# A two-token attention decode step: one load stream through a ring of 2-MB slots, and PE work interleaved by groups of eight

## The chip, the core and the metric

The kernel runs on one core of a Trainium2 chip. The metric is device time in microseconds (us) of one execution. Engines are named as the profile names them: PE (matmuls; PEld is its weight load), DVE, ACT, POOL, and SP, which here only issues transfers. Sixteen DMA engines move the data between HBM and the core's memory (SBUF); matmuls write to PSUM.

## The reference

```python
def _A_ref(x, k_cache, v_cache, wq, wo):          # x 2x1x512, caches 2x32x8192x128
    q = (x @ wq).reshape(B, Sq, H, Dh)            # heads H = 32, Dh = 128
    scores = einsum("bhqd,bhkd->bhqk", q, k_cache) * (Dh ** -0.5)
    o = einsum("bhqk,bhkd->bhqd", softmax(scores), v_cache)
    return o.reshape(B, Sq, H * Dh) @ wo
...
def _B_ref(x, w1, w2):                            # w1 512x1792, w2 1792x512
    return relu(x @ w1) @ w2
...
xn = layernorm(x)
return x + _A_ref(xn, k_cache, v_cache, wq, wo) + _B_ref(xn, w1, w2)
```

All arrays are bf16. The two caches are 2 x 134 MB and are read once. The weights wq and wo have 4.19 MB each, w1 and w2 1.84 MB each.

## The kernel before

There are 64 pairs of batch and head, called heads below. The cache of one head is one transfer of 2 MB for K and one of 2 MB for V, 16 KB per partition, both issued by SP (`issue_k_dma`, `issue_v_dma`). K has 3 buffers and V has 4. The weights and x are issued by ACT, wq and w1 at the start, w2 and wo after the first products with them.

A head takes these steps. `transpose_phase` turns 64 blocks of K on PE (`tp`, L204) in 8 groups of 8, and each group is copied from PSUM to SBUF (`kt_`), six by DVE and two by ACT. `qk_phase` multiplies each turned block with the query, written 64 times side by side (`qbt`), so the 64 matmuls have 64 columns (`S`, L235), and takes the row maximum (`mcol`). `stats_tr` turns that column on PE (`tr`) and DVE takes the maximum (`mx`). `stats_exp` spreads it over the partitions by a matmul (`bcp`), ACT negates it (`NM`) and takes the exponential with its row sums (`Psb`, `RS`). `stats_den` sums over the partitions on PE (`dbp`), and DVE takes the reciprocal (`RD`). `pv_phase` runs 64 matmuls of V with the probabilities (`ot`, L283), and ACT scales the result (`OTn`). `wo_phase` multiplies with that head's part of wo into one accumulator (`fin`, L299). After all heads, 14 matmuls add the second product of B (L328), DVE adds x (`osb`), and SP writes it out.

The loop `for it in range(NBH + 3)` calls the phases of up to four heads, but the order of the instructions on an engine is set by a scheduler when the kernel is built, not by this text.

Of the kernel before, what the change touches and what calls it, by code (L numbers as in the profile page):

```python
# [24 lines left out]
def kernel(  # L25
# [33 lines left out]

    const = ctx.enter_context(tc.tile_pool(name="const", bufs=1))  # L60
    wbig = ctx.enter_context(tc.tile_pool(name="wbig", bufs=1))
    wff = ctx.enter_context(tc.tile_pool(name="wff", bufs=1))
    kpool = ctx.enter_context(tc.tile_pool(name="kpool", bufs=K_BUFS))
    vpool = ctx.enter_context(tc.tile_pool(name="vpool", bufs=V_BUFS))
    kts = ctx.enter_context(tc.tile_pool(name="kts", bufs=KTS_BUFS))
    small = ctx.enter_context(tc.tile_pool(name="small", bufs=4))
    psT = ctx.enter_context(tc.tile_pool(name="psT", bufs=PST_BUFS, space=bass.MemoryType.PSUM))
    psS = ctx.enter_context(tc.tile_pool(name="psS", bufs=1, space=bass.MemoryType.PSUM))
    psO = ctx.enter_context(tc.tile_pool(name="psO", bufs=1, space=bass.MemoryType.PSUM))
    psM = ctx.enter_context(tc.tile_pool(name="psM", bufs=1, space=bass.MemoryType.PSUM))  # L70
    psF = ctx.enter_context(tc.tile_pool(name="psF", bufs=1, space=bass.MemoryType.PSUM))

    ksb_tiles = {}
    vsb_tiles = {}

    def issue_k_dma(bh):
        if bh >= NBH:
            return
        b, h = bh // H, bh % H
        ksb = kpool.tile([P, KB, Dh], bf16, name="ksb")  # L80
        nc.sync.dma_start(
            ksb[:], A_k_cache[b, h].rearrange("(m kk) d -> m kk d", m=P)
        )
        ksb_tiles[bh] = ksb

    def issue_v_dma(bh):
        if bh >= NBH:
            return
        b, h = bh // H, bh % H
        vsb = vpool.tile([P, KB, Dh], bf16, name="vsb")  # L90
        nc.sync.dma_start(
            vsb[:], A_v_cache[b, h].rearrange("(m kk) d -> m kk d", m=P)
        )
        vsb_tiles[bh] = vsb
# [19 lines left out]
    nc.scalar.dma_start(w1_sb[:], B_w1.rearrange("(kt p) f -> p kt f", p=P))

    for bh in range(PF):
        issue_k_dma(bh)
        issue_v_dma(bh)

    stats = const.tile([Bsz, nc.vector.BN_STATS_DIM], f32, name="stats")  # L120
# [247 lines left out]
```

## Time and profile before

| | |
|---|---|
| timed runs | 733.4, 733.94 and 735.46 us; median 733.94 us |
| the profiled execution, first to last instruction (its span) | 731.9 us |
| between that span and the median of the runs | 2.0 us |
| PE busy | 580.9 us (79% of the span) |
| DVE, ACT busy | 292.6 us (40%), 192.4 us (26%) |
| moved by DMA | 282.25 MB, 386 GB/s over the span |

No own time of the profiled execution stands beside its span, so the 2.0 us to the median are taken as what lies around it. The busy shares are means over the span; where a stage waits is seen in the chain of work and in the windows.

### The profile page before, as it was taken

Reading aid. Unit: us, or ns where it says so; the run is one execution under the profiler, and the core shown is the slowest. Engines: PE = TensorE matmul, PEld = TensorE weight load, DVE = VectorE, ACT = ScalarE, POOL = GpSimd, SP = SyncE. Lnnn points to the kernel's source line nnn. Section 1 sums busy time; section 2 is a strip of 40 time slices with the busy share of each in tenths; the row PEclk is TensorE's granted clock in tenths of the full one; section 3 lists DMA queues with packets and bytes.
Section 4 is the critical chain, followed back from the end, with each engine's and each line's share of the span. In section 5 each row is a group of like instructions: output and inputs, shape, how many; then the busy total and the mean of one; then the engine's idle time right before and its main releaser. Section 6 shows DMA issues by size and latency. Waiting matters only on the chain.

```text
span 731.9 us, 27513 instructions
## 1 busy us (share of the span) xinstructions
PE 580.9 (79%) x12810; PEld 531.1 (73%) x12810; DVE 292.6 (40%) x655; ACT 192.4 (26%) x433; POOL 4.5 (1%) x9
## 2 busy tenths in 40 slices
PE   3273998888888888888888888888888888888887
PEld 3262988778777877777777778777877777787775
DVE  3020454434334434443443344434434442444342
ACT  1032333222222222222222222222222222222221
POOL 2000000000000000000000000000000000000000
PEclk9565999999999999999999999999999999999999
DMA  9999999999999999999999999999999999999920
GB/s 368 429 420 372 370 424 428 424 426 424 407 407 411 408 388 394 396 399 409 390 424 417 363 385 417 402 394 420 399 392 383 407 405 402 373 416 415 398 118 2
DMA packets 25529, 282.25 MB, mean 386 GB/s; under 512 B 2116, under 2 KB 8008, under 8 KB 8520
## 3 DMA queue, kind: packets, MB, share of 16 engines
q1 hardware_dynamic: 18436, 268.45, 89.6%
q10 hardware_dynamic: 6980, 12.06, 4.6%
q8 instruction: 100, 1.64, 0.9%
q14 instruction: 13, 0.11, 0.0%
HBM read 280.50 MB, written 0.00 MB: 383 GB/s over the span
## 4 chain that ended last, share of the span: by engine, by line
PE 78%; ACT 8%; DMA 4%; DVE 4%; issue 4%; another core or an unknown queue 1%; ACTq 1%; DVEq 0%
PE tp L204 32%; PE ot L283 17%; PE S L235 17%; DMA wq_sb<-in_A_wq_dram 4%; ACT Psb L264 3%; PE dbp L275 3%; PE fin L299 3%; ACT OTn L290 2%; DVE mx L254 2%; PE tr L252 2%; DVE mcol L244 2%; ACT NM L263 1%; PE bcp L262 1%; PE qp L169 1%
## 5 line engine op out<-in xcount | busy, mean ns | idle before, releaser
L204 PE MATMUL tp<-identb,ksb 128*128 128x128 bf16 x4096 | 252.7, 223 | 22.2 <-DMA ksb<-in_A_k_cache_dram 19.2
L204 PEld LDWEIGHTS <-ksb 128*128 128x128 bf16 x4096 | 236.5, 100 | 36.9 <-DMA ksb<-in_A_k_cache_dram 19.3
L283 PE MATMUL ot<-Psb,vsb 128*128 128x64 bf16 x4096 | 136.4, 193 | 2.5 <-issue 2.5
L283 PEld LDWEIGHTS <-vsb 128*128 128x128 bf16 x4096 | 133.6, 99 | 3.6 <-issue 2.8
L275 PEld LDWEIGHTS dbp<-RS,onesf 128*128 128x128 f32 x128 | 19.3, 189 | 73.8 <-ACT Psb L264 73.1
L275 PE MATMUL dbp<-RS,onesf 128*128 128x1 f32 x128 | 24.6, 261 | 44.7 <-ACT Psb L264 43.7
L290 ACT ACTIVATE OTn<-ot,RD 128x1 bf16<-128x1 f32 x64 | 16.9, 263 | 150.5 <-PE ot L283 150.5
L276 DVE RECIPROCAL RD<-dbp 128x1 f32<-128x1 f32 x64 | 10.8, 168 | 106.7 <-PE dbp L275 106.7
L244 DVE TENSOR_REDUCE mcol<-S 128x1 bf16<-128x64 f32 x64 | 14.5, 227 | 89.3 <-PE S L235 89.3
L299 PE MATMUL fin<-wo_sb,OTn 128*2 128x512 bf16 x64 | 25.1, 393 | 20.3 <-ACT OTn L290 19.1
L263 ACT ACTIVATE NM<-bcp 128x1 f32<-128x1 f32 x64 | 10.9, 170 | 111.0 <-PE bcp L262 106.4
L254 DVE TENSOR_REDUCE mx<-tr 1x1 bf16<-1x128 bf16 x64 | 17.9, 280 | 31.1 <-PE tr L252 31.1
L252 PE MATMUL tr<-identb,mcol 128*1 128x128 bf16 x64 | 13.9, 218 | 20.0 <-DVE mcol L244 19.7
L262 PE MATMUL bcp<-mx,onesb 1*128 1x1 bf16 x64 | 10.2, 160 | 20.7 <-DVE mx L254 20.0
L299 PEld LDWEIGHTS <-OTn 128*2 128x2 bf16 x64 | 5.1, 79 | 28.4 <-ACT OTn L290 26.5
L252 PEld LDWEIGHTS <-mcol 128*1 128x1 bf16 x64 | 5.1, 79 | 27.3 <-DVE mcol L244 26.5
L264 ACT ACTIVATE Psb<-S,NM 128x64 bf16<-128x64 f32 x64 | 20.2, 316 | 2.5 <-ACT NM L263 0.5
L223 DVE TENSOR_SCALAR qbt<-onesq,qT 128x64 bf16<-128x64 bf16 x64 | 14.8, 232 | 7.5 <-ACT qT L176 7.4
L169 PEld LDWEIGHTS <-wq_sb 128*128 128x128 bf16 x128 | 7.9, 109 | 10.0 <-DMA wq_sb<-in_A_wq_dram 6.3
L169 PE MATMUL qp<-xnT,wq_sb 128*128 128x2 bf16 x128 | 8.1, 167 | 8.3 <-DMA wq_sb<-in_A_wq_dram 6.1
L264 ACT ACTIVATION_READ_ACCUMULATOR Psb<-S,NM 128x1 f32 x64 | 12.3, 193 | 0.0
L176 ACT COPY qT<-qp 128x2 f32<-128x2 f32 x32 | 5.1, 161 | 27.2 <-PE qp L169 27.2
(1567 smaller groups left out, 794.0 us busy)
## 6 DMA issues: line engine op xcount, KB each, us to landing
ksb<-in_A_k_cache_dram SPq DMA_DIRECT2D x64, 2048.0 KB, 10.1
vsb<-in_A_v_cache_dram SPq DMA_DIRECT2D x64, 2048.0 KB, 14.8
wq_sb<-in_A_wq_dram ACTq DMA_DIRECT2D x1, 4096.0 KB, 32.8
wo_sb<-in_A_wo_dram ACTq DMA_DIRECT2D x1, 4096.0 KB, 23.7
w_sb<-in_B_w_dram ACTq DMA_DIRECT2D x2, 1792.0 KB
xsb<-in_A_x_dram ACTq DMA_DIRECT2D x1, 2.0 KB
out_dram<-osb SPq DMA_DIRECT2D x1, 2.0 KB
```

The source lines that it names most:

```text
L169: nc.tensor.matmul(qp[:], lhsT=wq_sb[:, kt, h * Dh:(h + 1) * Dh], rhs=xnT[:, kt, :], start=(kt == 0), stop=(kt == KT_ - 1),)
L204: nc.tensor.transpose(tp[:, i, :], ksb[:, kk, :], identb[:])
L235: nc.tensor.matmul(S[:, j, kk:kk + QN], lhsT=kt_[:, i, :], rhs=qbt[:], start=True, stop=True,)
L244: nc.vector.tensor_reduce(out=mcol[:], in_=Sj, axis=AX.X, op=ALU.max)
L252: nc.tensor.transpose(tr[:], mcol[:], identb[:])
L254: nc.vector.tensor_reduce(out=mx[:], in_=tr[:], axis=AX.X, op=ALU.max)
L263: nc.scalar.mul(NM[:, bh:bh + 1], bcp[:], -1.0)
L264: nc.scalar.activation(out=Psb[:, bh, 0:KB], in_=Sj, func=ACTF.Exp, bias=NM[:, bh:bh + 1], scale=1.0, accum_out=RS[:, bh:bh + 1],)
L275: nc.tensor.matmul(dbp[:], lhsT=onesf[:, :], rhs=RS[:, bh:bh + 1], start=True, stop=True)
L283: nc.tensor.matmul(ot[:], lhsT=vsb[:, kk, :], rhs=Psb[:, bh, kk:kk + PN], start=(kk == 0), stop=(kk == KB - 1),)
L290: nc.scalar.activation(out=OTn[b][:, h, b:b + 1], in_=ot[:, 0:1], func=ACTF.Copy, scale=RD[:, bh:bh + 1],)
L299: nc.tensor.matmul(fin[:], lhsT=OTn[b][:, h, :], rhs=weights2["wo"][:, h, :], start=(bh == 0), stop=False,)
```

## The change

All large loads are issued by SP, in one fixed order (`stream`): both halves of wq; then K of head 0, 1 and 2 with V of head 0 behind K of head 2, and from there K of head i before V of head i-2; last wo in two halves, w1 and w2. Each load takes one of 11 slots of 2 MB (`ring`), whatever it carries. Load n is issued once load n-11 has been used for the last time (`pump`, `done`). x is still issued by ACT. wq, w1 and w2 are split over the partitions so that a partition's rows lie side by side in memory; wo is read in 1-KB rows as before.

The order on the engines is now that of the text (`manual_schedule`). The main loop goes by groups of eight blocks: it turns group G, multiplies group G-2 with the query, and multiplies group G-16 (two heads back) with V. The column maximum is turned once in a head, and the probabilities are made two groups later. The queries are no longer written out 64 times: the matmuls read one column 64 times over (`to_broadcast`), and so do those with V. ACT copies three of eight groups, not two. The denominators are taken once at the end by one matmul for all heads, and the products with wo, the first product of B and the second one come after the last head.

```diff
-QN = int(os.environ.get("DEV_QN", "64"))
-PN = int(os.environ.get("DEV_PN", "64"))
-PST_BUFS = int(os.environ.get("DEV_PST", "4"))
-KTS_BUFS = int(os.environ.get("DEV_KTS", "8"))
-K_BUFS = int(os.environ.get("DEV_KB", "3"))
-V_BUFS = int(os.environ.get("DEV_VB", "4"))
-ACT_EVERY = int(os.environ.get("DEV_ACTEVERY", "4"))
-PF = int(os.environ.get("DEV_PF", "2"))
+SLOTS = 11
+EG = 8
+LAG_S = 2
+LAG_PV = 16
+VLAG = 2
+WIDE = 64
...
+    ring = ctx.enter_context(tc.tile_pool(name="ring", bufs=SLOTS))
+    kts = ctx.enter_context(tc.tile_pool(name="kts", bufs=LAG_S + 2))
+    small = ctx.enter_context(tc.tile_pool(name="small", bufs=3))
+    psT = ctx.enter_context(tc.tile_pool(name="psT", bufs=3, space=PS))
+    psS = ctx.enter_context(tc.tile_pool(name="psS", bufs=2, space=PS))
+    psO = ctx.enter_context(tc.tile_pool(name="psO", bufs=2, space=PS))
+    psM = ctx.enter_context(tc.tile_pool(name="psM", bufs=1, space=PS))
+    ctx.enter_context(tc.manual_schedule())
...
+    def load_wq(i):
+        t = slot("wq_sb")
+        v = A_wq.rearrange("(p kt) n -> p kt n", kt=KT)
+        half = KT // 2
+        nc.sync.dma_start(
+            t[:].rearrange("p (kt n) -> p kt n", kt=half),
+            v[:, i * half:(i + 1) * half, :],
+        )
...
+    def load_k(bh):
+        t = slot("ksb")
+        nc.sync.dma_start(
+            t[:].rearrange("p (kk d) -> p kk d", d=Dh),
+            A_k_cache[bh // H, bh % H].rearrange("(m kk) d -> m kk d", m=P),
+        )
+        return t
...
+    def load_wo(i):
+        t = slot("wo_sb")
+        hh = H // 2
+        v = A_wo.rearrange("(h d) n -> d h n", d=Dh)
+        nc.sync.dma_start(
+            t[:].rearrange("p (h n) -> p h n", n=D), v[:, i * hh:(i + 1) * hh, :]
+        )
+        return t
+    def load_w2(_):
+        t = slot("w2_sb")
+        v = B_w2.rearrange("(p j) n -> p j n", j=FT)
+        s = t[:, 0:FT * D].rearrange("p (j n) -> p j n", n=D)
+        cut = FT - 2
+        nc.sync.dma_start(s[:, 0:cut, :], v[:, 0:cut, :])
+        nc.sync.dma_start(s[:, cut:FT, :], v[:, cut:FT, :])
+        return t
+    stream = [("wq", 0), ("wq", 1)]
+    for i in range(NBH + VLAG):
+        if i < NBH:
+            stream.append(("k", i))
+        if i >= VLAG:
+            stream.append(("v", i - VLAG))
+    stream += [("wo", 0), ("wo", 1), ("w1", 0), ("w2", 0)]
+    loaders = dict(wq=load_wq, k=load_k, v=load_v, w1=load_w1, wo=load_wo, w2=load_w2)
+    pos = [0]
+    def pump():
+        while pos[0] < len(stream):
+            n = pos[0]
+            if n >= SLOTS and not freed.get(stream[n - SLOTS]):
+                return
+            kind, i = stream[n]
+            live[(kind, i)] = loaders[kind](i)
+            pos[0] += 1
+    def done(key):
+        freed[key] = True
+        pump()
...
+    xsb = const.tile([Bsz, D], bf16, name="xsb")
+    nc.scalar.dma_start(xsb[:], A_x.flatten_outer_dims())
+    pump()
...
+    def q_proj():
+        qp = psM.tile([P, H, Bsz], f32, name="qp", tag="m")
         for h in range(H):
...
+        nc.vector.tensor_scalar(
+            out=qb[:], in0=qp[:], scalar1=inv_sqrt, scalar2=None, op0=ALU.mult
+        )
+        done(("wq", 0))
+        done(("wq", 1))
+    def transposes(G):
+        bh, e = G // NG, G % NG
+        ksb = live[("k", bh)]
+        tp = psT.tile([P, EG, P], bf16, name="tp")
+        for i in range(EG):
+            kk = e * EG + i
+            nc.tensor.transpose(tp[:, i, :], ksb[:, kk * Dh:(kk + 1) * Dh], identb[:])
+        kt_ = kts.tile([P, EG, P], bf16, name="kt_")
+        if e % 3 == 1:
+            nc.scalar.copy(kt_[:], tp[:])
+        else:
+            nc.vector.tensor_copy(kt_[:], tp[:])
+        kt_of[G] = kt_
+        if e == NG - 1:
+            done(("k", bh))
+    def scores(G):
+        bh, e = G // NG, G % NG
         b, h = bh // H, bh % H
...
+        if e == 0:
+            s_of[bh] = psS.tile([P, KB + WIDE], f32, name="S")
+        S = s_of[bh]
+        kt_ = kt_of.pop(G)
+        for i in range(EG):
+            kk = e * EG + i
+            nc.tensor.matmul(
+                S[:, kk:kk + WIDE],
+                lhsT=kt_[:, i, :],
+                rhs=qb[:, h, b:b + 1].to_broadcast([P, WIDE]),
+                start=True,
+                stop=True,
+            )
+        if e == NG - 1:
+            mcol = small.tile([P, 1], bf16, name="mcol", tag="mcol")
+            nc.vector.tensor_reduce(out=mcol[:], in_=S[:, 0:KB], axis=AX.X, op=ALU.max)
+            mcol_of[bh] = mcol
...
+        nc.tensor.transpose(tr[:], mcol_of.pop(bh)[:], identb[:])
+        mx = small.tile([1, 1], bf16, name="mx", tag="mx")
+        nc.vector.tensor_reduce(out=mx[:], in_=tr[:], axis=AX.X, op=ALU.max, negate=True)
...
+    def soft(bh):
+        b, h = bh // H, bh % H
...
+        nc.tensor.matmul(bcp[:], lhsT=onesb[:], rhs=mx_of.pop(bh)[:], start=True, stop=True)
+        nm = small.tile([P, 1], f32, name="nm", tag="nm")
+        nc.scalar.copy(nm[:], bcp[:])
+        pr = small.tile([P, KB], bf16, name="pr", tag="pr")
         nc.scalar.activation(
...
+            out=pr[:],
+            in_=s_of.pop(bh)[:, 0:KB],
             func=ACTF.Exp,
...
+            bias=nm[:],
             scale=1.0,
...
+            accum_out=RS[:, h, b:b + 1],
+        )
+        p_of[bh] = pr
+    def weighted(G):
...
+        vsb = live[("v", bh)]
+        if e == 0:
+            o_of[bh] = psO.tile([P, WIDE], f32, name="ot")
+        ot = o_of[bh]
+        pr = p_of[bh]
+        for i in range(EG):
+            kk = e * EG + i
             nc.tensor.matmul(
                 ot[:],
...
+                lhsT=vsb[:, kk * Dh:(kk + 1) * Dh],
+                rhs=pr[:, kk:kk + 1].to_broadcast([P, WIDE]),
                 start=(kk == 0),
                 stop=(kk == KB - 1),
...
+        if e == NG - 1:
+            nc.scalar.copy(OTf[:, h, b:b + 1], ot[:, 0:1])
+            p_of.pop(bh)
+            o_of.pop(bh)
+            done(("v", bh))
...
+    NT = NBH * NG
+    q_proj()
+    for G in range(NT + LAG_PV):
+        if G < NT:
+            transposes(G)
+        if LAG_S <= G < NT + LAG_S:
+            scores(G - LAG_S)
+        if G >= LAG_PV:
+            weighted(G - LAG_PV)
+        g = G - LAG_S - NG
+        if g >= 0 and g % NG == 0 and g // NG < NBH:
+            max_row(g // NG)
+        g = G - LAG_S - NG - 2
+        if g >= 0 and g % NG == 0 and g // NG < NBH:
+            soft(g // NG)
...
+    dbp = psM.tile([P, H, Bsz], f32, name="dbp", tag="m")
+    nc.tensor.matmul(
+        dbp[:].rearrange("p h b -> p (h b)"),
+        lhsT=onesf[:],
+        rhs=RS[:].rearrange("p h b -> p (h b)"),
+        start=True,
+        stop=True,
+    )
+    RD = const.tile([P, H, Bsz], f32, name="RD")
+    nc.vector.reciprocal(out=RD[:], in_=dbp[:])
+    OTn = const.tile([P, H, Bsz], bf16, name="OTn")
+    nc.vector.tensor_tensor(out=OTn[:], in0=OTf[:], in1=RD[:], op=ALU.mult)
+    fin = psO.tile([Bsz, D], f32, name="fin", tag="ot")
+    for h in range(H):
+        w = live[("wo", h // (H // 2))][:].rearrange("p (h n) -> p h n", n=D)
...
+            fin[:], lhsT=OTn[:, h, :], rhs=w[:, h % (H // 2), :], start=(h == 0), stop=False
+        )
...
+    w1 = live[("w1", 0)][:, 0:KT * Dff].rearrange("p (kt f j) -> p kt j f", kt=KT, j=FT)
+    hp = psM.tile([P, FT, Bsz], f32, name="hp", tag="m")
+    for j in range(FT):
+        for kt in range(KT):
+            nc.tensor.matmul(
...
+    nc.vector.tensor_scalar(out=hT[:], in0=hp[:], scalar1=0.0, scalar2=None, op0=ALU.max)
+    w2 = live[("w2", 0)][:, 0:FT * D].rearrange("p (j n) -> p j n", n=D)
+    for j in range(FT):
         nc.tensor.matmul(
...
+            fin[:], lhsT=hT[:, j, :], rhs=w2[:, j, :], start=False, stop=(j == FT - 1)
         )
```

The first place is SP at the start of the program. These are its first loads before; DMAHW0 to DMAHW7 stand for the completion of earlier transfers, PE for that of work on PE.

```order
L81 DMA ksb_115<-in_A_k_cache_dram 128x8192
L91 DMA vsb_117<-in_A_v_cache_dram 128x8192
L81 DMA ksb_119<-in_A_k_cache_dram 128x8192
L91 DMA vsb_121<-in_A_v_cache_dram 128x8192
L81 DMA ksb_157<-in_A_k_cache_dram 128x8192
L91 DMA vsb_527<-in_A_v_cache_dram 128x8192 [waits DMAHW0_49]
L81 DMA ksb_529<-in_A_k_cache_dram 128x8192 [waits DMAHW2_49,DMAHW1_49,PE_49]
```

And these now:

```order
L75 DMA wq_sb_83<-in_A_wq_dram 128x8192
L75 DMA wq_sb_85<-in_A_wq_dram 128x8192
L83 DMA ksb_87<-in_A_k_cache_dram 128x8192
...
L91 DMA vsb_93<-in_A_v_cache_dram 128x8192
L83 DMA ksb_95<-in_A_k_cache_dram 128x8192
L91 DMA vsb_97<-in_A_v_cache_dram 128x8192 [waits DMAHW0_49]
L83 DMA ksb_99<-in_A_k_cache_dram 128x8192 [waits DMAHW1_49]
...
L91 DMA vsb_266<-in_A_v_cache_dram 128x8192 [waits DMAHW4_49,PE_49]
```

wq, which was ACT's, has moved into SP's queue ahead of the caches. Eight completion semaphores go round, so a load waits until the one issued eight before it has landed, and from the twelfth on also for PE to have used its slot.

The second place is PE in the middle of the program, from the last group of scores of a head to its first matmul with V (before):

```order
L235 LDWEIGHTS kt__9909 [waits Activation_49]
L235 MATMUL S_9993<-qbt_9994,kt__9909 128x64
...
L252 LDWEIGHTS mcol_10060 [waits DVE_49]
L252 MATMUL tr_10150<-identb_91,mcol_10060 1x128
L262 LDWEIGHTS onesb_103
L262 MATMUL bcp_10220<-mx_10152,onesb_103 128x1 [waits DVE_49]
L275 MATMUL dbp_10229<-RS_152,onesf_101 128x1 [waits Activation_49]
L283 LDWEIGHTS vsb_9510 [waits DMAHW6_49]
L283 MATMUL ot_10392<-Psb_149,vsb_9510 128x64
```

And a group of the changed kernel, at the first group of a head:

```order
L221 LDWEIGHTS ksb_8799 [waits DMAHW5_49]
L221 MATMUL tp_9976<-identb_105,ksb_8799 128x128 [waits PE_49]
...
L240 LDWEIGHTS kt__9926 [waits DVE_49]
L240 MATMUL S_9809<-qb_132,kt__9926 128x64
...
L286 LDWEIGHTS vsb_9015 [waits DMAHW6_49]
L286 MATMUL ot_9995<-pr_9888,vsb_9015 128x64 [waits Activation_49]
```

Before, four waits for DVE and ACT stood one behind the other between the scores and the matmuls with V of a head. Now eight blocks of each kind follow one another, of three different heads, and a head's first group waits for its K and for the V of two heads back.

The third place is SP's last rows now; before, it had only K, V and the output there, and the weights were ACT's.

```order
L91 DMA vsb_13969<-in_A_v_cache_dram 128x8192
L91 DMA vsb_14185<-in_A_v_cache_dram 128x8192
L109 DMA wo_sb_14204<-in_A_wo_dram 128x16x512
L109 DMA wo_sb_14420<-in_A_wo_dram 128x16x512
L99 DMA w1_sb_14439<-in_B_w1_dram 128x7168
L119 DMA w2_sb_14655<-in_B_w2_dram 128x6144
L120 DMA w2_sb_14655<-in_B_w2_dram 128x1024
L356 DMA out_0_dram<-osb_15408 2x512
```

The weights of the last products now come after the last V.

## Rows read from the trace of the kernel before

**Rows 1.** The page: span, PE clock, DMA share and GB/s in 40 slices.
```profile
span 731.9 us, 27513 instructions
...
PEclk9565999999999999999999999999999999999999
DMA  9999999999999999999999999999999999999920
GB/s 368 429 420 372 370 424 428 424 426 424 407 407 411 408 388 394 396 399 409 390 424 417 363 385 417 402 394 420 399 392 383 407 405 402 373 416 415 398 118 2
DMA packets 25529, 282.25 MB, mean 386 GB/s; under 512 B 2116, under 2 KB 8008, under 8 KB 8520
```

**Rows 2.** Waits, PE's and SP's: us in total, times, longest us.
```profile
PE tp L204 <- DMA ksb<-in_A_k_cache_dram: 19.2, 2, 10.2
...
SPq L81 <- PE tp L204: 481.2, 51, 10.9
```

**Rows 3.** The chain of work, 461 to 485 us: start, us, what.
```profile
462.61 3.68 PE tp L204 x64
466.29 1.91 PE S L235 x64
...
469.56 0.41 ACT Psb L264 x2
...
470.40 1.95 PE ot L283 x64
...
473.06 3.68 PE tp L204 x64
```

**Rows 4.** The chain of work, 88 to 108 us.
```profile
88.73 0.61 PE tp L204 x9
...
94.63 0.15 PE tr L252
...
96.78 0.11 PE bcp L262
...
97.19 0.61 PE tp L204 x9
```

**Rows 5.** Windows: us, busy us (instructions) by engine, granted PE clock, DMA share, GB/s.
```profile
0.00:5.00 5.00, 0.00 (x0) 0.00 (x0) 1.32 (x8) 1.58 (x2) 4.45 (x9) 1.00 0.67 210
...
65.00:79.00 14.00, 7.76 (x140) 7.45 (x140) 4.78 (x11) 3.88 (x6) 0.00 (x0) 0.60 1.13 349
...
100.00:120.00 20.00, 17.97 (x413) 16.83 (x411) 9.96 (x23) 5.51 (x12) 0.00 (x0) 1.00 1.01 428
...
120.00:140.00 20.00, 16.43 (x381) 14.80 (x378) 7.68 (x19) 5.62 (x12) 0.00 (x0) 1.00 1.00 424
...
160.00:175.00 15.00, 11.84 (x270) 10.45 (x267) 5.28 (x14) 3.59 (x10) 0.00 (x0) 1.00 1.01 424
...
400.00:500.00 100.00, 83.45 (x1898) 77.17 (x1897) 44.65 (x98) 27.81 (x56) 0.00 (x0) 1.00 0.99 396
```

**Rows 6.** Windows of 1 us in one head's turn; K is issued at 466.32.
```profile
464.00:465.00 1.00, 1.00 (x21) 1.00 (x19) 1.00 (x2) 0.46 (x1) 0.00 (x0) 1.00 1.00 426
...
468.00:469.00 1.00, 0.40 (x8) 0.23 (x4) 0.55 (x3) 0.00 (x0) 0.00 (x0) 1.00 0.77 262
```

**Rows 7.** K transfers issued from 120 to 160 us: size, us from issue to landing.
```profile
ksb<-in_A_k_cache_dram SPq DMA_DIRECT2D x4, 2048.0 KB, 15.9
```

**Rows 8.** K transfers of the whole span: the page's row of DMA issues.
```profile
ksb<-in_A_k_cache_dram SPq DMA_DIRECT2D x64, 2048.0 KB, 10.1
```

**Rows 9.** Costliest groups: busy us and mean ns of one; the small products.
```profile
L169 PE MATMUL qp<-xnT,wq_sb 128*128 128x2 bf16 x128 | 8.1, 167 | 8.3 <-DMA wq_sb<-in_A_wq_dram 6.1 <-ACT qT L176 2.2
...
L181 PE MATMUL hp<-xnT,w_sb 128*128 128x2 bf16 x56 | 3.5, 166 | 9.2 <-DMA w_sb<-in_B_w_dram 5.8 <-ACT hT L188 3.4
```

**Rows 10.** The timeline of the end: start, us, engine, what.
```profile
725.91 3.18 PE L328 MATMUL fin<-w_sb,hT 128*2 128x512 bf16 x14
729.13 0.68 DVE L336 TENSOR_TENSOR osb<-fin,xsb 2x512 bf16<-2x512 f32 x1 [5.51 <-PE fin L328]
729.83 0.33 SPq L337 DMA_DIRECT2D out_dram<-osb  x1
```

More of the change, by code (lines that the diff above doesn't have):

```diff
@@ L62 @@
[L62 to L68, printed above, removed]
@@ L81, in issue_k_dma, with slot @@
+    def slot(name):
+        return ring.tile([P, SLOT], bf16, name=name, tag="slot")
+    def load_wq(i):
+        t = slot("wq_sb")
+        v = A_wq.rearrange("(p kt) n -> p kt n", kt=KT)
+        half = KT // 2
         nc.sync.dma_start(
-            ksb[:], A_k_cache[b, h].rearrange("(m kk) d -> m kk d", m=P)
-        )
[L84 to L90, printed above, removed]
+            t[:].rearrange("p (kt n) -> p kt n", kt=half),
+            v[:, i * half:(i + 1) * half, :],
+        )
+        return t
@@ L114 @@
[L114 to L118, printed above, removed]
     stats = const.tile([Bsz, nc.vector.BN_STATS_DIM], f32, name="stats")
@@ L141 @@
     )
-    xnT = const.tile([P, KT_, Bsz], bf16, name="xnT")
-    for kt in range(KT_):
-        tpx = psM.tile([P, Bsz], bf16, name="tpx", tag="m")
-        nc.tensor.transpose(tpx[:], xn[:, kt * P:(kt + 1) * P], identb[0:Bsz, 0:Bsz])
-        nc.vector.tensor_copy(xnT[:, kt, :], tpx[:])
-    OTn = [const.tile([P, H, Bsz], bf16, name=f"OTn{b}") for b in range(Bsz)]
-    for b in range(Bsz):
-        nc.vector.memset(OTn[b][:], 0.0)
-    Psb = const.tile([P, NBH, KB + PN - 1], bf16, name="Psb")
@@ new lines @@
+    tpx = psM.tile([P, KT, Bsz], bf16, name="tpx", tag="m")
+    for kt in range(KT):
+        nc.tensor.transpose(tpx[:, kt, :], xn[:, kt, :], identb[0:Bsz, 0:Bsz])
+    nc.vector.tensor_copy(xnT[:], tpx[:])
+    qb = const.tile([P, H, Bsz], bf16, name="qb")
+    hT = const.tile([P, FT, Bsz], bf16, name="hT")
+    RS = const.tile([P, H, Bsz], f32, name="RS")
+    OTf = const.tile([P, H, Bsz], f32, name="OTf")
+    kt_of = {}
+    s_of = {}
+    p_of = {}
+    o_of = {}
+    mcol_of = {}
+    mx_of = {}
@@ L172, in q_and_ffn_hidden @@
                     rhs=xnT[:, kt, :],
                     start=(kt == 0),
[L174 removed]
+                    stop=(kt == KT - 1),
                 )
[L176 to L188 removed]
@@ L273, in stats_den @@
-    def stats_den(bh):
-        dbp = psM.tile([P, 1], f32, name="dbp", tag="m")
-        nc.tensor.matmul(dbp[:], lhsT=onesf[:, :], rhs=RS[:, bh:bh + 1], start=True, stop=True)
-        nc.vector.reciprocal(out=RD[:, bh:bh + 1], in_=dbp[:])
-    def pv_phase(bh):
-        b, h = bh // H, bh % H
-        vsb = vsb_tiles[bh]
-        ot = psO.tile([P, PN], f32, name="ot")
-        for kk in range(KB):
+        nc.vector.tensor_scalar(
+            out=qb[:], in0=qp[:], scalar1=inv_sqrt, scalar2=None, op0=ALU.mult
+        )
@@ L327 @@
-    for f in range(FT):
-        nc.tensor.matmul(
-            fin[:],
-            lhsT=hT[:, f, :],
-            rhs=weights2["w2"][:, f, :],
-            start=False,
-            stop=(f == FT - 1),
+        if e == NG - 1:
[18 more added lines that the diff above has]
+            soft(g // NG)
@@ new lines @@
+    for h in range(H):
+        w = live[("wo", h // (H // 2))][:].rearrange("p (h n) -> p h n", n=D)
+        nc.tensor.matmul(
+            fin[:], lhsT=OTn[:, h, :], rhs=w[:, h % (H // 2), :], start=(h == 0), stop=False
+        )
+    w1 = live[("w1", 0)][:, 0:KT * Dff].rearrange("p (kt f j) -> p kt j f", kt=KT, j=FT)
+    hp = psM.tile([P, FT, Bsz], f32, name="hp", tag="m")
+    for j in range(FT):
+        for kt in range(KT):
+            nc.tensor.matmul(
+                hp[:, j, :],
+                lhsT=w1[:, kt, j, :],
+                rhs=xnT[:, kt, :],
+                start=(kt == 0),
+                stop=(kt == KT - 1),
+            )
```

212 lines of the change are left out of this document (36 added, 176 removed).

## The prediction

> **What bounds the kernel now.** First look at the forty slices of the page [rows 1]. The DMA share reads 9 nearly everywhere, as though the loads were the limit. But the GB/s below it are not even: 420 to 428 in the slices from about 90 to 180 us, then about 400 to the end of the loads. The waits show who holds back whom [rows 2]. PE waited for K only twice in the whole span, 19.2 us in all, while SP stood 481.2 us before issuing K because PE had not yet finished with a buffer. So from some 180 us on the loads are paced by PE.
>
> The chain of work shows PE's pace [rows 3]. The transposes of successive heads start at 462.61 and 473.06, 10.45 us apart. Of this the three blocks of 64 matmuls take 3.68 + 1.91 + 1.95 = 7.54 us. The other 2.91 us are a relay between engines, in which PE does almost nothing: S ends at 468.20, and the matmuls with V start at 470.40, after maximum, transpose, maximum, broadcast, negation, exponential (ACT Psb at 469.56) and denominator. The instructions alone don't force that. Around 90 us the same work of a head, in another order, took 97.19 - 88.73 = 8.46 us with PE never waiting [rows 4], and there the loads were the limit.
>
> The slower DMA rate of the later stage is then a result and not a cause. In the turn of a head the rate is 426 GB/s in one microsecond and 262 in another, 2 us after K was issued at 466.32 [rows 6]: the queue is nearly empty when the next load comes, and some of the engines stand. The share of 0.99 doesn't tell it, so packets that are held up seem to count as busy. When more loads were queued, K took 15.9 us to land (median of four [rows 7]), against 10.1 over the whole span [rows 8], and all four windows from 100 to 175 us moved 424 to 428 GB/s [rows 5].
>
> **What the change does to this.** Bytes: the same arrays are read once, 282.25 MB with the instructions [rows 1].
>
> *PE.* The relay leaves the path: a head's scores, its maximum, its exponential and its products with V now lie several groups apart, with other heads' matmuls between. What a head still costs PE is 3.68 + 1.91 + 1.95 + 0.15 + 0.11 = 7.80 us [rows 3, 4]; the denominators and wo go to the end. 64 heads make 499 us. A head's 4.19 MB at 425.6 GB/s (the mean of the windows 428, 424, 426 and 424, by their lengths [rows 5]) take 9.86 us. The loads become the bound, with 2.06 us in hand for each head. DVE and ACT are no bound: they were busy 9.96 and 5.51 us in 20 us at the faster stage [rows 5], in which some two heads passed (413 PE instructions, 197 to a head); ACT gets one copy more.
>
> *The ring.* Eight loads can be under way, so the queue holds up to 8 x 4.93 = 39 us of work. A slot must be free 11 loads later, 54 us; K's is free when PE has turned it, V's one head's PE time (7.8 us) after V landed. That is far from dry, at the start too: wq (4.19 MB) lands at about 14 us, the query products take 8.1 us of PE [rows 9], K of head 0 is used up by about 30 us, and its slot is asked for only after 13 loads, 64 us. That all large loads are in one queue costs nothing: the windows from 100 to 175 us had K and V alone, in SP's queue.
>
> *Unknown: the repeated column.* Matmuls that read one column 64 times don't occur before. The likely price is that of a 64-column matmul, 1.91 / 64 = 30 ns [rows 3]. From below I see no gain; from above I take the 128-column row, 3.68 / 64 = 57.5 ns. I take 30 ns, since the count of columns is the same. Up to 46 ns the loads hide it: (9.86 - 0.26 - 3.68) / 128.
>
> **The sum.** In the first 5 us, 210 GB/s were moved [rows 5], which is 2.5 us lost. wo, 4.19 MB in 1-KB rows, goes at the 349 GB/s of the window in which w2 and wo were read in such rows: 12.0 us. The other 278.06 MB at 425.6 GB/s take 653.4 us. The last byte moves at 2.5 + 653.4 + 12.0 = 667.9 us.
>
> Behind it lies a tail, because the weights come last. w1 is through when only the 1.84 MB of w2 are left, 4.3 us earlier, at 663.6. From the end of a transfer to its use I allow 2.1 us, the whole time from the issue of the output (729.83 [rows 10]) to the end of the span (731.9): 665.7. Then 56 products with w1, 3.5 us [rows 9], 0.3 us on DVE, 14 matmuls with w2, the sum on DVE 0.7 and the output 2.1. The 14 matmuls took 3.2 us at the full clock [rows 10]. [...] The end is 665.7 + 3.5 + 0.3 + 6.4 + 0.7 + 2.1 = 678.7 us. The products with wo (32, at 0.22 to 0.44 us) fit in the 20 us between the last V and the last byte.
>
> The span of the profiled execution, 731.9 us, lies 2.0 us below the median of the runs, 733.94; with this the forecast is 680.7, and I say 680 us, 7.3% less. Its own range is 671 (428 GB/s throughout, the tail at the full clock, and a load usable sooner than allowed) to 693 (a mean of 418 GB/s).
>
> **The rivals.**
>
> *The DMA engines themselves are slower later on.* If the 396 to 405 GB/s after 200 us [rows 1, 5] were their own limit and not PE's pace, 278.06 MB at 396 take 702.2 us, and the time is 680.7 + 702.2 - 653.4 = 729.5; at 405 GB/s 713.9. Against it: the dips stand just behind each issue, and 426 is reached between them [rows 6]. For it: no stage of the trace shows 425 for longer than the 75 us from 100 to 175. In its share I count smaller losses of rate too.
>
> [...]
>
> [...]
>
> [...]
>
> **How the numbers follow.** The forecast gets 0.78. Slower DMA engines, or another loss that leaves 693 to 731, get 0.12. The clock gets 0.03 and the repeated column 0.05, both slower. That gains and losses cancel within 0.3%, about what a measurement of this kernel can tell from no change, gets 0.02. So faster has 0.90, same 0.02, slower 0.08. The range from 671 to 712 us holds nearly all of the first case and about half of the second, some 8 in 10.
>
> **What the changed profile would show.** If right: GB/s of 420 and more in all slices from the second to the last V, and the lower rate of wo just before the end; K some 39 us from issue to landing; SP waiting for earlier loads more than for PE; PE waiting for ksb or vsb about 2 us in each head, 130 us in all; PE clock near 1.0 in the middle; about 11 us from the last byte to the end. If wrong: slices near 400 GB/s although PE waits for loads (the DMA engines' own rate), or PE busy without a gap and heads over 9.9 us apart, with matmuls of S or ot further apart than 30 ns (the repeated column) or a clock well under 1 (the clock). A ring that runs dry would show as SP waiting for PE and a K landing in 10 us.

## The result and the profile after

The changed kernel takes 688.32 us (median of 4 runs, 688.12 to 689.56), the kernel before 734.69 us beside it (733.4 to 735.46). The ratio is 0.937, with an interval of 0.9346 to 0.9394. Forecast were 680 us; the direction and the cause hold, and the time is 8 us above the forecast. The profiled execution was the slowest of the four, 689.56 us, and its span is 687.7.

First the page of the changed kernel: span, granted clock and GB/s in 40 slices, the queue that carries instructions, and the landing of K (last column, median us).

```profile
span 687.7 us, 27103 instructions
...
PEclk9999999999999999999999999989999999999998
...
GB/s 370 432 422 423 426 426 423 427 426 424 425 425 425 424 425 426 425 424 425 425 427 421 424 428 423 425 424 426 424 425 426 425 425 426 423 426 426 311 303 135
...
q8 instruction: 99, 1.62, 1.0%
...
ksb<-in_A_k_cache_dram SPq DMA_DIRECT2D x64, 2048.0 KB, 40.6
```

From the second slice to the 37th there are now 421 to 432 GB/s, where before they fell to about 400 [rows 1]. So the DMA engines had no lower rate of their own later on. K lands 40.6 us after its issue (39 were expected, 10.1 before [rows 8]). Only the last three slices are uneven: there stands the difference to the forecast.

The waits say the same from the other side (columns: us in all, times, longest).

```profile
PE ot L286 <- DMA vsb<-in_A_v_cache_dram: 93.8, 59, 3.3
...
SPq L83 <- DMA ksb<-in_A_k_cache_dram: 274.8, 59, 6.0
SPq L91 <- DMA vsb<-in_A_v_cache_dram: 273.1, 59, 5.9
...
SPq L83 <- PE tp L221: 8.9, 37, 0.4
```

PE waits for V once in a head, 1.6 us; SP waits for earlier loads, and for PE's transposes only 8.9 us, where it was 481.2 [rows 2]. The roles are exchanged: PE waits for the loads.

How much that is worth is read from one instruction that occurs once in a head, the transpose of the maximum: 64 of them, from the first start to the last. The row of before, then that of the changed kernel:

```profile
L252 PE MATMUL tr<-identb,mcol x64: 217/217/264, 64.8 to 721.6; 128*1 128x128 bf16 x64
```

```profile
L254 PE MATMUL tr<-identb,mcol x64: 217/217/266, 27.3 to 656.7; 128*1 128x128 bf16 x64
```

Before, a head took (721.6 - 64.8) / 63 = 10.43 us, now 9.99. That is 27 us over 63 heads. The first head is through 37.5 us sooner, since wq now comes first and w1, with B's products, no longer stands ahead of it; in return 31.0 us lie behind the last head instead of 10.3. Together 27.4 + 37.5 - 20.7 = 44.2 us, the difference of the spans.

The end of the loads, in windows of the changed kernel (busy us of PE, PEld, DVE, ACT, POOL with instruction counts; then clock, DMA share, GB/s):

```profile
644.00:648.00 4.00, 2.36 (x62) 2.24 (x59) 1.28 (x2) 1.07 (x2) 0.00 (x0) 1.00 0.65 259
648.00:652.00 4.00, 4.00 (x100) 3.83 (x96) 1.84 (x4) 1.40 (x2) 0.00 (x0) 1.00 0.55 231
652.00:656.00 4.00, 3.88 (x98) 3.69 (x96) 1.38 (x2) 2.16 (x6) 0.00 (x0) 1.00 0.48 203
656.00:660.00 4.00, 3.26 (x93) 2.95 (x89) 0.51 (x2) 0.73 (x4) 0.00 (x0) 1.00 0.65 218
...
676.00:680.00 4.00, 3.72 (x45) 2.74 (x45) 0.19 (x1) 0.00 (x0) 0.00 (x0) 0.74 0.17 65
```

From 644 to 658 us the DMA share is near one half and the rate 203 to 259 GB/s, although weights are still to come. Half of the engines stand: when the 16-KB packets of K and V in the trace are strung end to start, they make 16 chains, of which eight end between 638 and 645 us and eight at 657. In the same stretch SP stood 29.4 us on the issue of the second half of wo (start, duration):

```profile
628.22 29.44 SPq L109 DMA_DIRECT2D wo_sb<-in_A_wo_dram  x1
```

So there were two theories: some engines are behind in their own rows of K and V (H), or SP's held issue starves the rest (I).

The tail, from the timeline (start, duration):

```profile
674.93 3.52 PE L341 MATMUL hp<-xnT,w_sb 128*128 128x2 bf16 x56 [0.69 <-DMA w_sb<-in_B_w_dram]
...
678.73 6.13 PE L351 MATMUL fin<-w_sb,hT 128*2 128x512 bf16 x14 [0.28 <-DVE hT L348]
...
684.89 0.68 DVE L355 TENSOR_TENSOR osb<-fin,xsb 2x512 bf16<-2x512 f32 x1 [6.22 <-PE fin L351]
```

This is the tail of the sum, term by term: 3.52 (forecast 3.5), 6.13 at a granted clock of 0.51 (6.4), 0.68, and 2.1 from the end of the sum (685.57) to the end of the span.

### The profile page after: what moved, and what is told of

It reads as the page before. It is cut to its first block, busy times and chain, and to the rows that moved or that the text cites. A ratio compares the mean times of both kernels' runs of the same rounds, so it can differ in the third digit from the quotient of the medians.

```text
span 687.7 us, 27103 instructions
## 1 busy us (share of the span) xinstructions
PE 565.5 (82%) x12652; PEld 532.8 (77%) x12652; DVE 254.5 (37%) x461; ACT 231.4 (34%) x451; POOL 0.7 (0%) x6
## 3 DMA queue, kind: packets, MB, share of 16 engines
q8 instruction: 99, 1.62, 1.0%
## 4 chain that ended last, share of the span: by engine, by line
DMA 96%; PE 3%; SPq 0%; issue 0%; ACT 0%; DVE 0%
DMA vsb<-in_A_v_cache_dram 93%; DMA w_sb<-in_B_w_dram 2%; PE fin L351 1%; PE hp L341 1%; PE tp L221 1%; PE ot L286 0%; PE S L240 0%; SPq L83 0%; ACT kt__15118 L224 0%; SPq L75 0%; SPq L91 0%; DVE osb L355 0%; PE tr L254 0%; PE bcp L262 0%; DVE hT L348 0%
## 5 line engine op out<-in xcount | busy, mean ns | idle before, releaser
L221 PE MATMUL tp<-identb,ksb 128*128 128x128 bf16 x4096 | 324.0, 223 | 2.8 <-DMA ksb<-in_A_k_cache_dram 1.4
L286 PE MATMUL ot<-pr,vsb 128*128 128x64 bf16 x4096 | 213.4, 194 | 97.6 <-DMA vsb<-in_A_v_cache_dram 93.8
L221 PEld LDWEIGHTS <-ksb 128*128 128x128 bf16 x4096 | 243.9, 100 | 9.5 <-issue 2.5
L286 PEld LDWEIGHTS <-vsb 128*128 128x128 bf16 x4096 | 163.0, 99 | 104.7 <-DMA vsb<-in_A_v_cache_dram 101.6
L266 ACT ACTIVATE pr<-S,nm 128x64 bf16<-128x64 f32 x64 | 20.1, 314 | 2.1
L266 ACT ACTIVATION_READ_ACCUMULATOR pr<-S,nm 128x1 f32 x64 | 12.3, 193 | 0.0
L294 ACT COPY OTf<-ot 128x1 f32<-128x1 f32 x64 | 10.5, 165 | 3.9 <-PE ot L286 3.9
L333 PE MATMUL fin<-wo_sb,OTn 128*2 128x512 bf16 x32 | 8.6, 428 | 3.5 <-DMA wo_sb<-in_A_wo_dram 3.5
L264 ACT COPY nm<-bcp 128x1 f32<-128x1 f32 x64 | 10.6, 165 | 1.8 <-PE bcp L262 1.8
L351 PE MATMUL fin<-w_sb,hT 128*2 128x512 bf16 x14 | 6.1, 628 | 0.3 <-DVE hT L348 0.3
## 6 DMA issues: line engine op xcount, KB each, us to landing
ksb<-in_A_k_cache_dram SPq DMA_DIRECT2D x64, 2048.0 KB, 40.6
vsb<-in_A_v_cache_dram SPq DMA_DIRECT2D x64, 2048.0 KB, 40.6
w_sb<-in_B_w_dram SPq DMA_DIRECT2D x1, 1792.0 KB, 17.1
```

Of the source, the lines that this page charges most:

```text
L221: nc.tensor.transpose(tp[:, i, :], ksb[:, kk * Dh:(kk + 1) * Dh], identb[:])
L264: nc.scalar.copy(nm[:], bcp[:])
L266: nc.scalar.activation(out=pr[:], in_=s_of.pop(bh)[:, 0:KB], func=ACTF.Exp, bias=nm[:], scale=1.0, accum_out=RS[:, h, b:b + 1],)
L286: nc.tensor.matmul(ot[:], lhsT=vsb[:, kk * Dh:(kk + 1) * Dh], rhs=pr[:, kk:kk + 1].to_broadcast([P, WIDE]), start=(kk == 0), stop=(kk == K ...
L294: nc.scalar.copy(OTf[:, h, b:b + 1], ot[:, 0:1])
L333: nc.tensor.matmul(fin[:], lhsT=OTn[:, h, :], rhs=w[:, h % (H // 2), :], start=(h == 0), stop=False)
```

## The experiments: where the gain comes from

**e4 and e9: the ring with the old order of PE.** Both keep a head's steps one behind the other on PE, as [rows 3] show them, and load through a ring of 8 slots. Edit, the same in both, written in short:

```
-    for G in range(NT + LAG_PV):
-        ...
+    for bh in range(NBH):
+        for e in range(NG): transposes(bh * NG + e)
+        for e in range(NG): scores(bh * NG + e)
+        max_row(bh); soft(bh); den(bh)
+        for e in range(NG): weighted(bh * NG + e)
+        wo_head(bh)
```

e4 left the copies as in the changed kernel (three buffers in PSUM, e % 3 == 1 on ACT).

> The load ring of the changed kernel with PE's order as it was before: for each head 64 transposes, 64 scores, maximum, exponential, denominator, 64 products with V, scaling and the product with wo, one after the other; wo is loaded early into buffers of its own, 8 slots remain, and the denominator and wo are taken in each head. If the relay between the engines bound the kernel before, heads are 10.4 us apart again in spite of the deep queue, and the time is 64 x 10.4 plus 28 us before the first head and 14 behind the last, about 705 to 735, with the loads near 400 GB/s. If the one deep queue brought the gain, it is 688 and the loads run at 425.

Measured: 808.37 us, ratio 1.1011 (1.0989 to 1.1033), slower than either theory allowed. The chain of e4 shows why the run doesn't isolate the order: the transposes themselves now wait for two copies in each head (start, duration).

```profile
403.94 1.02 ACT kt__7707 L231
...
405.64 1.02 ACT kt__7740 L231
```

e9 is e4 with four buffers in PSUM, every fourth copy on ACT, as before, and one S buffer.

> The ring (8 slots) with PE's order as the trace of before shows it in the middle: a head's transposes, scores, maximum, broadcast, denominator, products with V, product with wo, one after the other, with the same four PSUM buffers and the same share of copies on ACT as before. Theory A (the order): heads 10.3 to 10.6 us apart, time 712 to 735 us. Theory B (the deep queue): heads 9.9 us apart, time 686 to 697 us.

Measured: 736.13 us, ratio 1.0012 (0.9993 to 1.0032): no gain at all. Its heads stand (716.7 - 40.0) / 63 = 10.74 us apart, by the starts of the transposed maximum:

```profile
L261 PE MATMUL tr<-identb,mcol x64: 217/217/217, 40.0 to 716.7; 128*1 128x128 bf16 x64
```

The rate falls from 424 GB/s (100 to 200 us) to 395 (400 to 500 us), as the loads' lead over PE is used up by the ring's size. The first head is 24.8 us sooner than before, but the heads stand 10.74 us apart against 10.43, and more work lies behind the last one. With the relay in PE's order, one queue and a ring of 8 slots give nothing. The three edits between e4 and e9 are together worth 72 us; they were not separated.

**e5: whole phases instead of groups.** The ring, and PE in the order in which the loop of before is written (scores of n-1, transposes of n, products with V of n-2), with no interleaving by group (10 slots; the edit written in short):

```
+    for it in range(NBH + 2):
+        if 1 <= it <= NBH: scores of head it-1
+        if it < NBH: transposes of head it
+        if 1 <= it <= NBH: max_row(it - 1)
+        if it >= 2: products with V of head it-2
+        if 1 <= it <= NBH: soft(it - 1)
```

> The changed kernel with its ring (10 slots), its lag of two heads for V and its denominators and wo at the end, but PE's work in whole phases, in the order and with the copies of the kernel before: scores of head n-1, transposes of head n, maximum of n-1, products with V of n-2, exponential of n-1. If the interleaving by group is what makes PE keep up (theory A), the transposes of successive heads stand 10 to 10.5 us apart in the middle, with the relay from S to the products with V of about 2 us, less some 0.2 us for the denominators, and the time is 700 to 730 us. If a full queue ahead of PE is enough (theory B: PE only lost time since K came late or SP issued late), heads stand 9.9 us apart and the time is 686 to 692 us.

Measured: 688.65 us (687.86 to 689.67), ratio 0.9362 (0.9328 to 0.9397), the time of the changed kernel. The expectation tied "the order" to the groups, and there it was wrong: the written order of before already puts the next head's transposes between S and its exponential. The timeline shows the relay hidden behind 64 transposes and 64 products with V:

```profile
461.21 0.41 PE L240 MATMUL S<-qb,kt__10548 128*128 128x64 bf16 x8
462.18 3.75 PE L221 MATMUL tp<-identb,ksb 128*128 128x128 bf16 x64 [0.56 <-DMA ksb<-in_A_k_cache_dram]
465.86 0.22 PE L254 MATMUL tr<-identb,mcol 128*1 128x128 bf16 x1
467.06 2.15 PE L286 MATMUL ot<-pr,vsb 128*128 128x64 bf16 x64 [0.98 <-DMA vsb<-in_A_v_cache_dram]
469.14 0.17 PE L262 MATMUL bcp<-mx,onesb 1*128 1x1 bf16 x1
469.24 0.42 PE L240 MATMUL S<-qb,kt__10706 128*128 128x64 bf16 x8
469.50 0.41 PE L240 MATMUL S<-qb,kt__10717 128*128 128x64 bf16 x8
```

So the interleaving by group is not needed: this order, in which other heads' matmuls fill the relay, does as well. Before, the scheduler had undone the one that was written (e8 below).

**e8: that order alone, without the ring.** The kernel before with one line more:

```
+    ctx.enter_context(tc.manual_schedule())
```

> The kernel before with one line more, which keeps every engine's instructions in the order in which the loops write them; its seven buffers, its two queues, its weights early, its denominators and its products with wo head by head stay. If PE's order is what cost the time (theory A), the relay is gone from the middle, heads stand 9.9 us apart, the K loads are queued and land in 15 us or more, and the time is 680 to 700 us, without the ring. If the deep queue of the ring is needed as well (theory B), the loads stay at about 400 GB/s and the time is 710 to 735 us.

Measured: 710.93 us (708.85 to 714.82), ratio 0.9686 (0.9648 to 0.9725). By its time it lies at the near edge of theory B's range, but what theory B said of the loads is not so: from 200 to 600 us they move at 418 to 425 GB/s. The pace is that of the changed kernel and of theory A, (699.0 - 71.2) / 63 = 9.97 us a head, but the first head is late, as the starts of the transposed maximum show, and then a window of the time ahead of it:

```profile
L253 PE MATMUL tr<-identb,mcol x64: 216/217/218, 71.2 to 699.0; 128*1 128x128 bf16 x64
```

```profile
53.00:71.00 18.00, 9.93 (x182) 9.13 (x183) 3.08 (x6) 3.42 (x15) 0.00 (x0) 0.61 0.46 163
```

From 53 to 71 us, while PE waits for w1 and makes B's products, the buffers are full and only 163 GB/s move. So the gain has two parts: PE's order (10.43 to 9.97 us a head) and the loads' order (wq alone ahead of K and V, the weights behind), which against e8 starts the heads 43.9 us sooner and costs 19.0 at the end; the spans, 711.0 and 687.7, differ by 23.3 us.

**e3: 7 slots instead of 11.**

```
-SLOTS = 11
+SLOTS = 7
```

> The changed kernel with 7 slots, as many 2-MB buffers as K and V had before. If the gain comes from PE's order and the denominators, so that PE no longer holds the buffers long, 7 slots still keep four loads under way (34.5 us round, of which a K slot is held 12.7) and the time stays at 688 within 3 us. If the gain comes from the depth of the ring, it falls back towards 734: over 705.

Measured: 688.26 us, ratio 0.9377 (0.9354 to 0.9399). SP now waits for PE (549.9 us for tp), K lands in 28.0 us, and nothing is lost. The depth beyond 7 slots is worth nothing.

## The experiments: the end of the loads

**e1: wo in long rows.** Each partition reads 32 whole rows of wo, 16 KB at a time (wo's rows are then in another order, so the output is another).

```
-        v = A_wo.rearrange("(h d) n -> d h n", d=Dh)
+        v = A_wo.rearrange("(d h) n -> d h n", d=Dh)
```

> The changed kernel with wo read in 16-KB rows (128 transfers rows of that size in each half, not 2048 rows of 1 KB); the rows of wo then lie in another order, so the last product is not the reference's, with the same number of instructions. Theory H (half of the 16 DMA engines are some 3% slower all along, so they finish their last K and V some 13 to 18 us after the others and set the end; the engines that stand from 644 to 658 us cost nothing): the idle stretch stays, only the slower 1-KB rows are saved, 2 x 128 x 50 ns against 16 x 617 ns on an engine, 3 us: 685 us. Theory I (the second half of wo holds SP in its issue for 29 us, and the engines run dry because w1 and w2 can't be issued): the stretch at 200 GB/s disappears and 8 to 10 us with it: 678 to 680 us.

Measured: 686.73 us, ratio 0.9356 (0.9335 to 0.9376). All loads are issued by 643 us, SP is held by none, and the stretch at half rate is still there, only later, as its windows show:

```profile
656.00:660.00 4.00, 3.28 (x93) 2.97 (x90) 0.51 (x2) 0.72 (x4) 0.00 (x0) 1.00 0.68 279
660.00:664.00 4.00, 1.68 (x40) 1.54 (x41) 0.78 (x2) 0.16 (x1) 0.00 (x0) 0.85 0.57 242
...
668.00:672.00 4.00, 4.00 (x16) 1.44 (x15) 0.00 (x0) 0.00 (x0) 0.00 (x0) 0.80 0.48 203
```

Theory I falls: SP's hold and the short rows are together worth about 1.6 us, the difference of the medians.

**e2, e6, e10: the same loads beside no, all, and half of the computation.** e2 loads and computes nothing. e6 makes the whole computation on a constant tile, so that PE waits for no load, and e10 half of the heads. No load waits for a slot (the first lines in all three, the last two in e6 and e10):

```
-            if n >= SLOTS and not freed.get(stream[n - SLOTS]):
-                return
...
-        ksb = live[("k", bh)]
+        ksb = fix
```

> The changed kernel's loads alone, same order, same slots, no PE, ACT or DVE work; the output is x plus some values of w2, read when the last load has landed. It leaves out the whole computation. Under both theories the loads bound the changed kernel, so the last load should land near 679 us and the time be about 682. If the slower half is slow because code for PE is fetched through the same engines (99 packets of 16 KB in the changed kernel), the halves end together here and the last load lands 8 to 14 us earlier: about 670. If the engines themselves differ, the rate falls to half for 10 us or more before the end here too. The rival that PE and not the loads set the pace would give far less, under 640.

> The loads of the changed kernel, held by nothing, beside its whole computation on a constant tile instead of what was loaded (the output is not the reference's). PE waits for no load, so its pace is its own: by the prediction 7.80 us a head, 499 us for 64 heads, and 9.9 us a head if PE's own work had been the limit. Of the end of the loads: if PE's instructions, fetched through the same 16 DMA engines, put half of the engines behind (theory H1), the instruction queue has 99 packets again, and the loads end at about 675 to 679 us, with a last stretch of some 15 us at half the rate; the time is 677 to 682 us. If what holds the loads up is that they wait for slots (theory H2), the loads run as alone, no stretch at half rate, and the time is 664 to 668 us.

> As the run with all loads and PE on a constant tile, but PE computes only 32 of the 64 heads (the output is not the reference's); the loads are the same. If the fetch of PE's instructions through the DMA engines makes half of them late (theory H1), there are about 50 instruction packets instead of 99, the stretch at half rate is half as long (7 us instead of 15), and the time is 672 to 677 us, between 665 with no instructions and 684 with all. If the stretch comes of how the queue is held or of wo's short rows beside a busy PE, whatever the number of instructions (theory H2), the time is 682 to 686 us, or 665 us.

Measured: 665.0, 684.03 and 674.92 us. The windows at the end of the loads, of e2, e6 and e10 in turn (in e2, only DVE and POOL have a column):

```profile
100.00:600.00 500.00, 0.00 (x0) 0.00 (x0) 1.00 1.01 428
...
656.00:660.00 4.00, 0.00 (x0) 0.00 (x0) 1.00 0.87 361
```

```profile
648.00:656.00 8.00, 0.00 (x0) 0.00 (x0) 0.00 (x0) 0.00 (x0) 0.00 (x0) 0.50 0.53 223
656.00:660.00 4.00, 0.00 (x0) 0.00 (x0) 0.00 (x0) 0.00 (x0) 0.00 (x0) 0.50 0.48 178
660.00:668.00 8.00, 0.00 (x0) 0.00 (x0) 0.00 (x0) 0.00 (x0) 0.00 (x0) 0.50 1.08 350
```

```profile
640.00:644.00 4.00, 0.00 (x0) 0.00 (x0) 0.00 (x0) 0.00 (x0) 0.00 (x0) 0.50 1.05 393
644.00:652.00 8.00, 0.00 (x0) 0.00 (x0) 0.00 (x0) 0.00 (x0) 0.00 (x0) 0.50 0.66 231
652.00:656.00 4.00, 0.00 (x0) 0.00 (x0) 0.00 (x0) 0.00 (x0) 0.00 (x0) 0.50 1.08 353
```

The instruction packets of e6 and e10 by their pages (packets, MB, share); e2's page has none in this queue:

```profile
q8 instruction: 99, 1.62, 1.0%
```

```profile
q8 instruction: 50, 0.82, 0.5%
```

With no computation there is no stretch at half rate; with all of it, some 14 us; with half of it, 8. The times stand at 665, 675 and 684, in equal steps, with 0, 50 and 99 instruction packets. In e10 PE had been idle for some 300 us when the stretch came, so what PE does at the end is not its cause: the lag was gathered on the way and shows when the queue runs out. PE's work on the tiles was halved together with the instruction packets, and no run separated the two, but the packets in the traces account for the lag. A 16-KB packet of K or V takes 0.61 us (median) in e6 as in e2. An instruction packet of the same size takes 1.07 us, and the packet of K or V behind it some 1.1. So each one costs its DMA engine 1.55 us beyond the loads: 153 us in all in e6, 77 in e10. The eight late engines end together 147 us later than the engines of e2 in e6, 73 in e10; the other eight end within some 5 us of e2's. Why half of the engines bear all of it stays open.

e6 also gives PE's own pace beside full loads, by the starts of the transposed maximum, and in its waits what holds PE up (us, times, longest):

```profile
L254 PE MATMUL tr<-identb,mcol x64: 216/217/218, 25.2 to 616.2; 128*1 128x128 bf16 x64
```

```profile
PE ot L286 <- issue: 27.7, 32, 1.6
PE S L240 <- issue: 24.8, 30, 1.5
PE tp L221 <- issue: 22.9, 30, 1.4
```

(616.2 - 25.2) / 63 = 9.38 us a head, not 7.80. PE stands 76 us in 93 waits for nothing that the profile names, 1.2 us a head. They are waits for its instructions: in the trace they stand 256 instructions apart or a multiple of it, and each ends 1.2 to 1.6 us after an instruction packet has come. The rest is in the matmuls, which keep PE busy for 87% of the time, 8.2 us a head.

**e7, e11, e12: a shorter tail.** e7 loads w1 and w2 near the start and wo three heads before the end; e11 loads all three by GpSimd's queue into buffers of their own. Both make 31 products with wo ahead of the last head's products with V:

```
+        if G - LAG_PV == NT - NG:
+            wo_products(0, H - 1)
         if G >= LAG_PV:
             weighted(G - LAG_PV)
```

> The changed kernel with w1 and w2 loaded near the start and B's products made at head 7, wo loaded three heads before the end and its products for 31 of the 32 heads made ahead of the last head's products with V, and the last V in four pieces. Behind the last byte only 16 products with V, a copy, a scaling, one product with wo, the sum and the output are left, about 5.5 to 6 us instead of 9. If the end of the loads stays where it is (some engines behind, whatever is loaded last), the time is 684 to 686 us. If the weights being last is what draws the end of the loads out (1-KB rows of wo with a queue that stands), the last byte comes 5 to 10 us earlier and the time is 673 to 680 us. If wo's issue now holds up SP in the middle and the ring runs dry, it is 690 or more.

> The changed kernel with w1, w2 and wo loaded from the fifth and the twenty-first head on by GpSimd's queue into buffers of their own, beside a ring of 7 slots that holds only wq, K and V, the last V in four pieces, and 31 of the 32 products with wo ahead of the last head's products with V. SP is held by no long issue. The last byte should come at about 674 to 678 us and 5.5 to 6 us lie behind it: 680 to 685 us. If the short rows of wo cost more where they share the engines with K and V, or PE (which has only some 0.4 us a head in hand beside its fetches) falls behind, it is 687 us or more.

Measured: 695.83 us (ratio 0.9457, 0.9427 to 0.9488) and 694.83 us (0.9464, 0.9444 to 0.9485), both slower than the changed kernel. In e7 the third case came true by its time and its hold: SP stood 30.7 us on the issue of wo's second half, K behind it came late, and from 620 to 630 us 228 GB/s moved. But the last byte came at 679.0 us all the same, and e11, which has no such hold, is only 1 us faster. The timeline of e11's end (start, duration) shows what both got wrong:

```profile
679.01 0.43 PE L336 MATMUL dbp<-RS,onesf 128*128 128x64 f32 x2
680.42 6.85 PE L350 MATMUL fin<-wo_sb,OTn 128*2 128x512 bf16 x31 [0.98 <-DVE OTn L345]
687.21 2.15 PE L290 MATMUL ot<-pr,vsb 128*128 128x64 bf16 x64
689.80 0.38 PE L350 MATMUL fin<-wo_sb,OTn 128*2 128x512 bf16 x1 [0.44 <-DVE OTn L345]
```

The last byte comes as early as ever, at 678.9 us, but PE is only then done with the head before the last, and 6.85 us of products with wo stand in front of the last V. In the changed kernel this work lies beside the loads of the weights. So "weights last" pays by what it covers.

e12 keeps that and turns only the order of the weights and of their products round, wo last and in six pieces:

```
-    stream += [("wo", 0), ("wo", 1), ("w1", 0), ("w2", 0)]
+    stream += [("w1", 0), ("w2", 0), ("wo", 0), ("wo", 1)]
```

> The changed kernel with the order of the last loads turned round: w1, w2, then wo, in six pieces, the last four of 512 KB each; B's products are made before those with wo. The last byte should come where it did, at about 679 us, since some engines set it whatever is loaded last. Behind it are now 4 products with wo (0.9 to 1.8 us), the sum and the output, about 6 us instead of 9, so 684.5 to 686.5 us. If the time stays at 688 or more, the tail behind the last byte was not what the last step of the sum said, or the short rows of wo at the very end cost more than they save.

Measured: 685.02 us (684.88 to 685.07), ratio 0.9326 (0.9304 to 0.9348), as expected, and the fastest complete version. Behind the last wait for a load stand now, in its timeline,

```profile
679.29 1.02 PE L353 MATMUL fin<-wo_sb,OTn 128*2 128x512 bf16 x4 [0.34 <-DMA wo_sb<-in_A_wo_dram]
...
680.35 0.68 DVE L358 TENSOR_TENSOR osb<-fin,xsb 2x512 bf16<-2x512 f32 x1 [13.27 <-PE fin L353]
```

and the output: 1.02 us of matmuls where 6.13 and 3.52 stood.

## Why the prediction held, and where it was off

- **PE's relay was the bound, the loads are now.** Right, and shown from both sides: e9 (relay with ring) 736 us, e5 (ring without relay) 689, e8 (no relay, no ring) 711 at the same pace a head as the changed kernel. A head takes 9.99 us, where 9.86 were worked out from 425.6 GB/s. The prediction credited PE's order and the deep queue together; the depth beyond 7 slots turned out to be worth nothing (e3), and the order of the loads 23 us against e8. In one sentence the prediction misread the trace of before: around 90 us the loads were not yet the limit, for from 88 to 97 us PE was busy for 9.00 of 9 us and the loads moved 395 GB/s.
- **The rate of the loads.** Right: 425 GB/s from 100 to 600 us. The rival of engines that are slower later on is excluded: 428 in e2.
- **The clock.** The forecast gave 0.03 to a fall of PE's clock that makes the change slower. The clock fell in small, and it cost nothing. Of the 25 windows of 20 us from 100 to 600 us, 11 have a granted clock of 0.90 to 0.96, as the first row below; the mean is 0.97. The trace's records of the clock have two levels, 1.00 and 0.50, so PE spent some 6% of this time at the lower one. Up to 620 us it fell ten times, each time 1.9 to 4.3 us after the start of a wait of PE of 2.8 to 3.3 us; the usual waits of 1.6 us, and one of 3.1, had no such end. A head with a fall takes 12.0 to 13.0 us, and the next one 8.1 to 9.0. In e6, where PE waits for no load (second row), the clock was 1.00 until PE's work ended. In e5, whose waits for V and K are 1.1 and 0.7 us in the mean, it was 0.988 over the whole profiled execution, where the changed kernel has 0.965; e5 takes the same time, since the loads are the bound. In the tail of the changed kernel the lower level came again, from 664.2 us, in a wait of 2.8 us for wo, and from 677.9.

```profile
120.00:140.00 20.00, 15.09 (x328) 14.54 (x325) 6.69 (x13) 5.65 (x10) 0.00 (x0) 0.91 1.01 424
```

```profile
100.00:200.00 100.00, 86.76 (x2059) 83.36 (x2056) 41.25 (x74) 37.73 (x77) 0.00 (x0) 1.00 1.01 425
```

- **The repeated column.** It costs what 64 written columns cost: blocks of 8 in the timeline of e5 (its last two rows above) and of the changed kernel follow each other in 0.25 us, 31 ns for a matmul. The price of 57.5 ns is excluded.
- **PE's reserve.** "2.06 us in hand for each head" was wrong by a factor of four: PE's own pace beside full loads is 9.38 us (e6), so about 0.5 us are left. The sum of matmul times left out the waits for instructions (1.2 us a head), and the matmuls took 8.2 us and not 7.80. It did not cost time here, since PE's waits for V take these up (93.8 us against the 130 expected).
- **The step that failed: "the last byte moves at 667.9 us".** Measured 678.8, the end of the last packet of w2. The sum divided all bytes by the rate of all 16 engines and so took it that all finish together. Half of them lag by some 12 to 19 us, as their instruction packets come on top, and the last loads, spread over all of them, end with the late half. The term grows by 10.9 us. The tail behind it, 10.8 expected, took 8.9: w1 was in use 0.5 us after its last byte and not 2.1. The 6.4 us for the 14 matmuls with w2 were the author's estimate, and no run shows them: the 14 took 3.18 us at a granted clock of 1.00 before and 6.13 at 0.51 now. Around the span lie 1.9 us, where 2.0 were expected, and the profiled execution is 1.2 us above the median. Together 10.9 - 1.9 - 0.1 - 1.2 = 7.7, the way from 680.7 to 688.3.

## What to carry to other kernels

Where PE looks busy and the loads look slow, compare the time between two heads with the sum of their matmul blocks: what is left over may be a relay; here two orders that put other heads' matmuls into it closed it, by groups or by whole phases, with no need for a deeper ring. In this kernel, bound by loads, the end was set by the DMA engines that were latest and not by the mean rate; and the last loads should be those that cover the work still queued on PE, with the least work behind the very last one.

## What the runs showed of the hardware

- PE's instructions come in packets through the same 16 DMA engines: 99 packets, 1.62 MB, for 25,304 instructions of PE, 256 each; a packet has 16 KB and takes 1.07 us (median). Running without a wait for data (e6), PE stood about 0.8 us for each, and each cost the loads 1.55 us of one DMA engine.
- Beside that work, the loads alone end 19 us later than without it (684.03 against 665.0 us), and 10 us later beside half of it.
- With earlier loads still queued, the second load in 1-KB rows held the queue that issues it: the first half of wo was issued in 0.39 us, the second in 29.4 (30.7 in e7) and the load behind it in 7.1 (5.7), against 0.33 us for 2 MB in 16-KB rows. At the very end this costs little (e1, 1.6 us); in e7, where loads of K stood behind it, PE waited 17.1 us for K, and the time is within 1 us of e11's all the same.
